# Five small moves in the routing work beside an attention loop on one Trainium2 core

## The chip, the core and the metric

The kernel runs on one core of one Trainium2 chip. TensorE (PE in the profile, with PEld for its weight loads), VectorE (DVE), ScalarE (ACT), GpSimd (POOL) and the DMA queues (SP's and others) each work through their own list of instructions in order, and wait for each other through semaphores. The metric is the device time of one execution in microseconds (us); lower is better.

## The reference

Two blocks follow each other. The first is a linear attention with a decaying state, for 4 batches, 8 heads, 768 tokens and 48 values a head; the second routes each token to one of 8 experts and applies that expert.

```
# attention, for every batch and head, t = 0..767
y[t]  = r[t] @ (state + (u*k[t])^T v[t]);  state = w[:,None]*state + k[t]^T v[t]
x     = y of the 8 heads side by side               # (4, 768, 384)
# routing and experts
logits = x @ w_gate (8 experts);  local = sigmoid(x @ w_local)
fresh  = argmax(logits)                              # first of equals
e[s]   = fresh if s == 0 or local < 0.5 else e[s-1]  # else keep the last token's expert
p      = softmax(logits)[e];  out = p * (relu(x @ w1[e]) @ w2[e])     # 384 -> 1024 -> 384
```

## The kernel before

**The attention loop.** `Attention.run` goes over 16 items (batch by head pair: n = 4*batch + pair, two heads at a time on 128 partitions) and one closing step. An item has 6 chunks of 128 tokens. Step n of the loop finishes item n-1 and begins item n, and it already computes the scores of item n+1. What belongs to one item:

- `load`: three DMAs on SP's queue (`rk`, `kv`, `vT`), four items ahead.
- `scale` on POOL: `rw` (r by powers of the decay), `ke` (k by powers of the decay), `pd` (r times k), two instructions each, one step ahead of their use. `keys` on DVE: `kw`, two steps ahead.
- `scores` on PE (L288), in two halves into two PSUM tiles of two banks each (`pair0`, `pair1`), which are taken in turn by everything that needs a bank; DVE masks each half into `am` (L290) and so frees the bank.
- `own` on PE (L267) into `y`, then DVE multiplies it by `vT` (L273). `inside` (L297) and `before` (L310) add the other two parts to `y`; ACT copies it to `xT` (L318). `turn` (L329) transposes it back into token order, and ACT copies that to `x` (L331).
- `added` on PE (L248) writes the states that the chunks add into `T`, and `states` on DVE (L254, a scan) runs over `T` and gives `S`, which `before` needs.

**The routing of the first two batches** ("group 0", 12 chunks) is put in pieces into steps 9 to 15 of the same loop (`g` is 8 in the code). `logits` and `token_logits` give `lt` at steps 8, 9, 12 and 13. `experts_of` finds the argmax (L688 to L696: maximum, comparison `eq`, product with `down`, maximum, key), `keys` transposes the keys (L703), `runs` is a running maximum that carries an expert forward (L708), `turn_runs` and `last` go back (L713, L720), `one_hot` ends it (L727 to L731). `counts` (L740, L741, PE) and `ranks` (L747 on ACT, L748 to L756 on DVE) number the tokens of each expert; `slots`, `columns` (`eqv`, L800), `places` (`ohq`, L811, two halves) and `numbers` (`val`, L805 on POOL) build the one-hot tables from which `summed` (L818, PE) makes the list of tokens for the first two experts. `head` (L828 to L849) ends with `gid`, by which POOL gathers rows of x from DRAM (L1077). After the loop the expert units follow, each a run of matmuls; they route the other two batches on their way.

**One PSUM bank for much.** `mp` is a single bank. It holds the tables of the first steps (columns 0 to 256), `T` (columns 258 to 497), the maximum `mx`, the transposed keys, and behind `T` (`mp[:, mp_end:]`) what `turn_runs` and `last` write. The tile library adds the semaphore waits, and it keeps two engines off one bank at the same time: a matmul that writes into `mp` waits for the DVE reads of `mp` that stand in front of it in the program, whatever their columns are.

**The order** is written out by hand: inside `tc.manual_schedule()` every engine's list has its instructions in the order in which the Python code issues them. So moving a line of `run` moves its instructions on each engine that it uses, and nothing else decides. `iota` makes small integer tables on POOL, and `cast` at step 6 turns some of them into floats on ACT.

Of the kernel before, what the change touches and what calls it, by code (L numbers as in the profile page):

```python
# [14 lines left out]
Alu = mybir.AluOpType  # L15
# [5 lines left out]
P = 128  # L21
# [5 lines left out]
E, F = 8, 1024  # L27
DK, FK = D // P, F // P
NCH = S // P
NC = B * NCH  # L30
N = B * S

ST = 4
# [4 lines left out]
EARLY = 2  # L38
HEAD = 192
TAIL = 256  # L40
# [15 lines left out]
def spread(ap, axis, n):  # L56

    a = ap.unsqueeze(axis)
    return a.to_broadcast([n if i == axis else s for i, s in enumerate(a.shape)])


class Attention:
# [289 lines left out]
    def run(self, router, fetch, heads):  # L352


        def pair(name):
            t = self.banks(name)
            return [t[:, 0], t[:, 1]]

        M = B * HP

        mp, mp_end = router.mp, 2 * P + 2 + (NCH - 1) * DH

        g = GROUPS[0][1] * HP
        for n in range(M + 1):
            if n + AHEAD - 1 < M:
                self.load(n + AHEAD - 1)
            if n == 0:
                self.scale(0)
                self.keys(0)
                self.tables()  # L370
                self.scores(0, 0)()
                self.scores(0, 1)()
                self.own(0)
                self.nc.scalar.copy(self.first, self.tab[:, 1, 0])
                self.turn_ends(slice(1, HP))
                self.warm(3)
                self.added(0)
                self.reciprocals(1)
                self.states(0)
                self.scale(1)  # L380
                continue
            if n < 3:

                self.keys(n)
                self.inside(n - 1)
                self.before(n - 1)
                if n == 2:
                    self.turn(0, pair("tp"))
                self.nc.scalar.copy(self.first, self.tab[:, n + 1, 0])
                self.scores(n, 0)()  # L390
                keep = self.scores(n, 1)
                self.own(n)
                keep()
                self.added(n)
                self.states(n)
                if n == 1:
                    self.reciprocals(2)
                self.scale(n + 1)
                continue
            if n < M:  # L400
                self.turn(n - 2, pair("tp"))
                if n >= M - 2:
                    fetch(2 * (n - M + 2))
                if n == 3:
                    self.reciprocals(3)
                if n < 5:
                    self.keys(n)
                if n > 3:
                    if n not in (g + 3, g + 5):
                        self.added(n)  # L410
                    self.states(n)
            if n == 4:
                self.keys(5)
            if n > HP and n % HP == 1:
                self.token_logits(n // HP - 1, pair("lq")[0])
            if n == g + 1:
                router.experts_of(0, (0,))
            if n == g + 5:
                router.slots(0)
                router.columns(0)  # L420
            if n == M:
                router.shares(0)
            if n + 1 < M:
                self.scale(n + 1)
            if n == g + 6:
                router.numbers(0, self.nc.gpsimd)
            if 3 <= n < 6:
                router.constants(n - 3)
            if n == M:
                self.turn(M - 2, [self.spare[:, 0], self.spare[:, 1]])  # L430
            self.inside(n - 1)
            if n == g + 3:

                router.turn_runs(0, mp[:, mp_end:])
            self.before(n - 1)
            if M - 2 <= n < M:
                fetch(2 * (n - M + 2) + 1)
            if n == 6:
                router.cast()
            if n == M:  # L440
                break
            if n == g + 3:
                router.last(0, mp[:, mp_end:])
                router.one_hot(0, (0,))
            if n == g + 7:

                router.summed(0, 0)
                router.copied(0, self.nc.vector.tensor_copy)
                self.spare = self.py.tile([P, 2, 512], F32, name="y")
                router.head(self.spare[:, 0])  # L450
                heads()

            ahead = n if n < 5 else n + 1
            if n == 3:
                self.added(3)
                self.states(3)
            if ahead < M:
                self.scores(ahead, 0)()
                keep = self.scores(ahead, 1)
            if n % HP == 0:  # L460

                keep()
                self.own(n)
                self.logits(n // HP - 1, pair("lp")[0])
                if n == 4:
                    self.scores(5, 0)()
                    self.scores(5, 1)()
                    self.keys(6)
                if n == g + 4:
                    self.added(n + 1)  # L470
                    router.counts(0, [mp, mp[:, E * NC // 2:]])
                    router.ranks(0, (0,))
                if n > 4:
                    self.keys(n + 2)
                if n == g + 4:
                    router.ranks(0, (1,))
            else:
                self.own(n)
                if n == g + 2:
                    self.added(n + 1)  # L480
                    router.keys(0, mp)
                    router.runs(0)
                if 4 < n < M - 2:
                    self.keys(n + 2)
                if ahead < M:
                    keep()
            if n == g + 1:
                router.experts_of(0, (1,))
            if n == g + 3:
                router.one_hot(0, (1,))  # L490
            if n == g + 5:
                router.places(0, 0)
            if n == g + 6:
                router.places(0, 1)
        self.inner.close()
# [81 lines left out]
class Router:  # L577
# [43 lines left out]
    def iota(self, name, shape, pattern, base=0, cm=0, cast=False):  # L621
# [5 lines left out]
        self.casts.append((f, i))  # L627
        return f

    def constants(self, part):  # L630
        nc = self.nc
        if part == 0:
            self.ie = self.iota("ie", [P, E], [[1, E]])
            self.iq = self.iota("iq", [P, P], [[1, P]])
            self.ij = self.iota("ij", [P, E * ST], [[1, E * ST]])
            self.ones = self.tl("r_ones", [P, P])
            nc.vector.memset(self.ones, 1.0)
        elif part == 1:
            self.down = self.iota("down", [P, E], [[-1, E]], base=E, cast=True)

            self.t8 = self.iota("t8", [P, NC], [[E * P, NC]], base=2 * E, cm=E, cast=True)
            self.t1 = self.iota("t1", [P, NC], [[P, NC]], base=1, cm=1, cast=True)
        else:

            c = self.g[0]["nc"]
# [5 lines left out]
            nc.vector.memset(self.go, 1.0)  # L651
            nc.vector.memset(self.go.rearrange("p (b c) -> p b c", c=NCH)[:, :, NCH - 1:], 0.0)
            nc.vector.memset(self.g[0]["ext"][:, :, 0:1], 0.0)

            self.tie = self.tl("tie", [P, E])
            for x, (z, base) in enumerate(((slice(0, EARLY), E - 1 - E * TAIL), (slice(EARLY, E), E - 1 - EARLY))):
                i = self.iota(f"tie{x}", [P, z.stop - z.start], [[-1, z.stop - z.start]], base=base)
                self.casts.append((self.tie[:, z], i))
            self.ief = self.iota("ief", [1, E], [[1, E]], cast=True)

            self.size = self.tl("size", [1, E])
            for i, n in enumerate(BLOCKS):
# [18 lines left out]
    def experts_of(self, i, parts=(0, 1)):  # L681

        nc, g, lt = self.nc, self.g[i], self.lt
        lg = lt[:, g["z"], :E]
        if 0 in parts:
            nc.vector.memset(lt[:, g["z"]].rearrange("p (b c) e -> p b c e", c=NCH)[0:1, :, 0, E:], -1.0)
            mx = self.mp[:, :g["nc"]] if i == 0 else g["mx"]
            nc.vector.tensor_reduce(mx, lg, axis=AX.X, op=Alu.max)  # L688
            nc.vector.tensor_tensor(g["eq"], lg, spread(mx, 2, E), op=Alu.is_equal)
            if i == 0:  # L690
                nc.scalar.copy(g["mx"], mx)
            nc.vector.tensor_tensor(g["eq"], g["eq"], spread(self.down, 1, g["nc"]), op=Alu.mult)
        if 1 in parts:
            nc.vector.tensor_reduce(g["k"], g["eq"], axis=AX.X, op=Alu.max)
            nc.vector.tensor_tensor(g["k"], self.t8[:, g["z"]], g["k"], op=Alu.subtract)
            nc.vector.scalar_tensor_tensor(g["key"], lt[:, g["z"], E], FRESH_TO, g["k"],  # L696
                                           Alu.is_le, Alu.mult)
# [1048 lines left out]
```

## Time and profile before

| what | value |
|---|---|
| time, 3 runs | median 382.65 us (382.16 to 382.88) |
| the profiled execution | 383.9 us, of which its span is 382.2 us |
| PE busy / PE weight loads | 367.5 us (96%) / 324.1 us (85%) |
| DVE / ACT / POOL busy | 250.6 us (66%) / 107.5 us (28%) / 151.3 us (40%) |
| attention loop | about 0 to 112 us of the span |
| expert units | about 112 to 373 us, PE busy throughout |

The profiled execution took 1.25 us more than the median of the timed runs. Times in the text are microseconds from the start of the span. A step of the loop is read best from one `before` (L310) to the next on PE. Busy PE does not mean PE at full rate: the granted clock of the array is given beside it.

### The profile page before, as it was taken

The page shows a single profiled execution, that of the slowest core. Times are in us where ns is not written, and L with a number is a line of the kernel's source. Part 1 is how long each engine was busy: PE and PEld are TensorE (multiplying, and loading weights), DVE is VectorE, ACT ScalarE, POOL GpSimd, SP SyncE. Part 2 cuts the span into 40 slices and gives each one's busy share as a digit, 9 for nine tenths or more (in the row PEclk, how much of TensorE's full clock was granted, in tenths as well). Part 3 has the DMA queues.
Part 4 walks back from the last instruction along what each step waited for, and adds up shares of the span by engine and source line. Part 5 has one row for each costly group of instructions (what it writes and reads, how often), then busy time and mean ns, then how long its engine had stood idle before and what let it go on. Part 6 is the DMA issues. An engine that isn't in the chain of part 4 may idle for free. (4 is left out here: it accounts for less than half of the span.)

```text
span 382.2 us, 9693 instructions
## 1 busy us (share of the span) xinstructions
PE 367.5 (96%) x3846; PEld 324.1 (85%) x3846; DVE 250.6 (66%) x720; ACT 107.5 (28%) x295; POOL 151.3 (40%) x213
## 2 busy tenths in 40 slices
PE   7999999989999999999999999999999999999992
PEld 6776777766769998999999999999998899899971
DVE  6888778967945746496566857758758758466400
ACT  4132232223222212322422333233234233232210
POOL 8779999867222042311422313212323113012022
PEclk9999999989999999999999999999999999999997
DMA  7999999972566881720551254145246156064011
GB/s 262 409 410 410 408 396 327 358 272 91 189 223 209 317 352 41 306 107 22 211 204 62 63 190 192 51 173 207 76 166 228 37 178 228 10 215 170 3 37 36
DMA packets 17765, 74.97 MB, mean 196 GB/s; under 512 B 2761, under 2 KB 6618, under 8 KB 15408
## 3 DMA queue, kind: packets, MB, share of 16 engines
q1 hardware_dynamic: 10336, 56.89, 39.9%
q0 software_dynamic: 3424, 9.52, 7.5%
q10 hardware_dynamic: 3952, 7.87, 5.7%
q8 instruction: 32, 0.52, 0.5%
q14 instruction: 21, 0.17, 0.1%
HBM read 64.83 MB, written 9.51 MB: 195 GB/s over the span
## 5 line engine op out<-in xcount | busy, mean ns | idle before, releaser
L1303 POOL DMA_INDIRECT out_dram<-yo,sid x27 | 26.6, 987 | 102.4 <-ACT yo L1298 79.0
L1154 PE MATMUL h<-exT,w1t 128*128 128x168 f32 (+4 forms) x240 | 54.9, 327 | 0.0
L1158 DVE TENSOR_TENSOR hT<-h,hs 128x168 f32<-128x168 f32 (+3 forms) x60 | 21.1, 351 | 46.5 <-PE h L1154 31.0
L1077 POOL DMA_INDIRECT xg<-x_d,gid x29 | 31.1, 1073 | 37.1 <-DVE sm L900 17.4
L1154 PEld LDWEIGHTS h<-exT,w1t 128*128 128x128 f32 x240 | 41.6, 190 | 0.3 <-issue 0.3
L1104 PE MATMUL h<-exT,w1t 128*128 128x192 f32 (+1 forms) x192 | 38.3, 338 | 0.0
L1223 PE MATMUL y<-factors,sums 128*128 128x192 f32 x168 | 36.8, 326 | 0.0
L216 POOL TENSOR_TENSOR pd<-rk 128x384 f32<-128x384 f32 x32 | 31.3, 999 | 10.2 <-PE y L267 7.6
L1154 PE MATMUL h<-xs,ws 128*128 128x168 f32 (+4 forms) x144 | 35.2, 326 | 0.0
L290 DVE TENSOR_TENSOR am<-pair,kept 128x768 f32<-128x768 f32 x32 | 30.0, 951 | 6.7 <-PE pair L288 6.1
L1104 PEld LDWEIGHTS h<-exT,w1t 128*128 128x128 f32 x192 | 32.3, 190 | 1.5 <-issue 0.2
L1154 PEld LDWEIGHTS h<-xs,ws 128*128 128x128 f32 x144 | 25.5, 190 | 4.3 <-ACT hs L1161 1.2
L1223 PEld LDWEIGHTS y<-factors,sums 128*128 128x128 f32 x168 | 28.9, 190 | 0.0
L212 POOL TENSOR_TENSOR ke<-kv,endT 128x288 f32<-128x288 f32 x32 | 25.0, 800 | 0.7 <-DMA kv<-in_kv_dram 0.7
L297 PE MATMUL y<-am,kv 128*64 128x128 f32 x360 | 23.9, 276 | 0.8 <-DVE y L273 0.8
L288 PE MATMUL pair<-rw,kw 48*64 48x128 f32 (+1 forms) x768 | 23.2, 253 | 1.4 <-DVE lt L349 0.6
L229 POOL TENSOR_TENSOR rw<-rk,tab 128x384 f32<-128x384 f32 x26 | 23.5, 924 | 2.1 <-DMA rk<-in_rk_dram 2.1
L1223 PE MATMUL y<-w2t,hT 128*128 128x192 f32 x96 | 23.0, 328 | 0.0
L288 PEld LDWEIGHTS pair<-rw,kw 48*64 48x64 f32 x768 | 19.7, 135 | 3.6 <-issue 1.2
L1091 DVE COPY exT<-tp 128x384 f32<-128x384 f32 (+6 forms) x29 | 14.0, 488 | 12.9 <-PE tp L1090 12.7
L297 PEld LDWEIGHTS y<-am,kv 128*64 128x64 f32 x360 | 20.0, 137 | 2.4 <-DVE y L273 1.0
L318 ACT COPY xT<-y 128x768 f32<-128x768 f32 x15 | 12.0, 801 | 34.0 <-PE y L310 34.0
(300 smaller groups left out, 740.4 us busy)
## 6 DMA issues: line engine op xcount, KB each, us to landing
w1t<-in_w_dram SPq DMA_DIRECT2D x8, 1536.0 KB, 6.6
w2t<-in_w_dram SPq DMA_DIRECT2D x8, 1536.0 KB, 7.1
rk<-in_rk_dram SPq DMA_DIRECT2D x15, 768.0 KB, 9.9
kv<-in_kv_dram SPq DMA_DIRECT2D x16, 584.0 KB, 8.4
vT<-in_vT_dram SPq DMA_DIRECT2D x16, 384.0 KB, 7.8
x_d<-x ACTq DMA_DIRECT2D x4, 1152.0 KB, 8.2
w1t<-in_w_dram SPq DMA_DIRECT2D x2, 768.0 KB, 4.6
w2t<-in_w_dram SPq DMA_DIRECT2D x2, 768.0 KB, 5.3
```

What stands on the lines that cost most here:

```text
L212: nc.gpsimd.tensor_mul(t["ke"][:, p::2], t["k"][:, p::2], spread(self.endT[:, p, hp], 1, C2))
L216: nc.gpsimd.tensor_mul(t["pd"][:, z], t["rT"][:, z], t["kT"][:, z])
L229: engine.tensor_mul(t["rw"][:, z], t["rT"][:, z], spread(pw, 1, z.stop - z.start))
L288: nc.tensor.matmul(sc[f * DP:(f + 1) * DP, h, i, x:], lhsT=t["kw"][q, c, o * DP:(o + 1) * DP], rhs=t["rw"][q, c, x:], start=True, stop=True)
L290: return lambda: nc.vector.tensor_mul(t["am"][:, g], sc, spread(self.kept[:, g:g + 3], 1, 2))
L297: nc.tensor.matmul(t["y"][h][p * DP:(p + 1) * DP, c2 * P:(c2 + 1) * P], lhsT=t["v"][:, (2 * c + h) * DH:(2 * c + h) * DH + DP], rhs=t["am" ...
L1077: self.nc.gpsimd.indirect_dma_start(out=xg[:n], out_offset=None, in_=self.x_d[:rows], in_offset=bass.IndirectOffsetOnAxis(ap=u["gid"][:n, ...
L1104: nc.tensor.matmul(h[:, :n], lhsT=u["w1"][:, m, kk, :], rhs=u["xT"][:, kk, :], start=(kk == 0), stop=(kk == DK - 1))
L1154: nc.tensor.matmul(out, lhsT=a, rhs=b, start=start and k == 0, stop=stop and k == len(terms) - 1, skip_group_check=True)
L1158: nc.vector.tensor_tensor(out, a, b, op=Alu.add)
L1223: return lambda: nc.tensor.matmul(bank[:, x * half:(x + 1) * half], lhsT=a, rhs=b, start=(j == 0 and x == 0), stop=(j == FK // 2 - 1), ski ...
L1303: self.nc.gpsimd.indirect_dma_start(out=out.rearrange("n (h d) -> (n h) d", h=2) if half else out, out_offset=bass.IndirectOffsetOnAxis(ap ...
```

## The change

Five moves, no new arithmetic:

1. In `experts_of` for group 0, the comparison `eq` is written into columns 12 to 107 of `mp` (PSUM), and its product with `down` reads it there; the product goes to the same SBUF tile as before.
2. The state scan of step 11 (`states(11)`) is issued in step 10, right behind `runs`, in place of its position at the start of step 11. On DVE it now stands in front of `kw` of item 12 and of the second `am` of item 11.
3. At step 12 `added(13)` and `counts` are issued in front of `logits` instead of behind it. `ranks` stays behind `logits`, so on ACT the copy `lT` of `logits` stays in front of the copy `ext` of `ranks`.
4. `eqv` moves from the start of step 13 to its end; the first half of `ohq` moves from the end of step 13 to step 14, behind its scan.
5. All nine `iota` tables are made on POOL at the end of step 2, in front of `scale(3)`, instead of in steps 3, 4 and 5.

```diff
@@ Attention.run
                 if n == 1:
                     self.reciprocals(2)
+                else:
+                    router.numbering()
                 self.scale(n + 1)
...
-                    self.states(n)
+                    if n != g + 3:
+                        self.states(n)
...
             if n == g + 5:
                 router.slots(0)
-                router.columns(0)
...
             if n == g + 6:
                 router.numbers(0, self.nc.gpsimd)
-            if 3 <= n < 6:
+                router.places(0, 0)
+            if n in (3, 5):
                 router.constants(n - 3)
...
                 self.own(n)
+                if n == g + 4:
+                    self.added(n + 1)
+                    router.counts(0, [mp, mp[:, E * NC // 2:]])
                 self.logits(n // HP - 1, pair("lp")[0])
...
                 if n == g + 4:
-                    self.added(n + 1)
-                    router.counts(0, [mp, mp[:, E * NC // 2:]])
                     router.ranks(0, (0,))
...
                     router.keys(0, mp)
                     router.runs(0)
+                    self.states(n + 1)
...
             if n == g + 5:
-                router.places(0, 0)
+                router.columns(0)
@@ Router (numbering() holds the iotas that constants() had)
+    def numbering(self):
+        self.ie = self.iota("ie", [P, E], [[1, E]])
+        self.iq = self.iota("iq", [P, P], [[1, P]])
+        self.ij = self.iota("ij", [P, E * ST], [[1, E * ST]])
+        self.down = self.iota("down", [P, E], [[-1, E]], base=E, cast=True)
+        self.t8 = self.iota("t8", [P, NC], [[E * P, NC]], base=2 * E, cm=E, cast=True)
+        self.t1 = self.iota("t1", [P, NC], [[P, NC]], base=1, cm=1, cast=True)
...
@@ Router.experts_of
-            nc.vector.tensor_tensor(g["eq"], lg, spread(mx, 2, E), op=Alu.is_equal)
+            eq = self.mp[:, g["nc"]:g["nc"] * (E + 1)].rearrange("p (c e) -> p c e", e=E) if i == 0 else g["eq"]
+            nc.vector.tensor_tensor(eq, lg, spread(mx, 2, E), op=Alu.is_equal)
             if i == 0:
                 nc.scalar.copy(g["mx"], mx)
-            nc.vector.tensor_tensor(g["eq"], g["eq"], spread(self.down, 1, g["nc"]), op=Alu.mult)
+            nc.vector.tensor_tensor(g["eq"], eq, spread(self.down, 1, g["nc"]), op=Alu.mult)
```

## The prediction

> **What bounds the kernel now.** I read the stages first (busy time by window: PE, weight loads, DVE, ACT, POOL, granted PE clock, DMA share, GB/s).
>
> ```profile
> 28.00:66.00 38.00, 37.16 (x814) 27.48 (x804) 30.01 (x59) 9.85 (x26) 38.00 (x52) 1.00 1.00 387
> 66.00:112.00 46.00, 42.48 (x889) 32.55 (x886) 36.27 (x59) 11.99 (x30) 28.56 (x33) 0.96 0.69 239
> 112.00:382.00 270.00, 262.82 (x1675) 243.92 (x1671) 161.78 (x557) 76.37 (x217) 63.78 (x89) 0.99 0.41 145
> ```
>
> From 112 us on PE never stops until the last sends, so whatever the loop ends earlier moves all of that forward. From 28 to 66 us PE has 0.84 us of gaps, though POOL is busy throughout: POOL is ahead (`rw(8)` ends at 51.39, its scores start at 54.10). All edits but the table move lie in 64 to 108 us, where PE has gaps and the clock falls below 1. The timelines of PE and DVE there (start, us, engine, line, what, idle before and its releaser):
>
> ```profile
> 69.46 0.80 PE L329 MATMUL pair<-ident,xT 112*128 112x112 f32 x6 [0.65 <-DVE am L290]
> 78.60 0.23 PE L713 MATMUL mp<-ident,run 12*128 12x12 f32 x1 [1.00 <-DVE inc L726]
> 95.55 0.77 PE L288 MATMUL pair<-rw,kw 48*64 48x128 f32 x24 [0.63 <-DVE lt L349]
> 97.69 0.79 PE L329 MATMUL pair<-ident,xT 112*128 112x112 f32 x6 [0.73 <-DVE am L290]
> ...
> 65.57 0.25 DVE L689 TENSOR_TENSOR eq<-lt,mp 128x96 f32<-128x96 f32 x1
> 65.86 2.67 DVE L692 TENSOR_TENSOR eq<-eq,down 128x96 f32<-128x96 f32 x1
> 68.46 0.94 DVE L290 TENSOR_TENSOR am<-pair,kept 128x768 f32<-128x768 f32 x1
> 75.87 0.40 DVE L708 TENSOR_TENSOR_SCAN run<-mp,seg 12x128 f32<-12x128 f32 x1
> 76.20 0.92 DVE L236 TENSOR_TENSOR kw<-rk,inv 128x768 f32<-128x768 f32 x1
> 77.05 0.94 DVE L290 TENSOR_TENSOR am<-pair,kept 128x768 f32<-128x768 f32 x1
> 77.92 0.63 DVE L254 TENSOR_TENSOR_SCAN S<-step,mp 128x240 f32<-128x240 f32 x1
> ...
> 116.14 0.26 DVE L692 TENSOR_TENSOR eq<-eq,down 128x96 f32<-128x96 f32 x1
> ```
>
> Three things are to be seen. L692 takes 2.67 us at 65.86 and 0.26 at 116.14, with the same shape. L713 starts when the scan S has ended (78.55), not when `run` has (76.27): it writes the bank that S reads; the name L726 is only DVE's next instruction. And DVE runs without a pause from 64.31 to 78.56, so there its order decides. The clock stands right behind L713's gap:
>
> ```profile
> 79.00:80.00 1.00, 1.00 (x26) 0.83 (x25) 0.00 (x0) 0.33 (x2) 1.00 (x2) 1.00 1.08 353
> 80.00:81.00 1.00, 1.00 (x42) 1.00 (x46) 0.76 (x4) 0.72 (x2) 0.06 (x1) 0.77 0.89 347
> 81.00:82.00 1.00, 1.00 (x22) 0.61 (x16) 0.72 (x1) 0.00 (x0) 0.00 (x0) 0.50 1.00 413
> 82.00:83.00 1.00, 1.00 (x9) 0.21 (x2) 0.04 (x1) 0.00 (x0) 0.00 (x0) 0.50 0.88 361
> 83.00:84.00 1.00, 1.00 (x6) 0.83 (x5) 1.00 (x2) 0.00 (x0) 0.98 (x2) 0.52 0.28 105
> 84.00:85.00 1.00, 1.00 (x29) 0.94 (x30) 1.00 (x2) 0.70 (x2) 1.00 (x3) 1.00 0.19 22
> ```
>
> **Comparison in PSUM (step 9).** During L692 POOL runs `rw` and `ke` without a break:
>
> ```profile
> 65.23 1.67 POOL L229 TENSOR_TENSOR rw<-rk,tab 128x384 f32<-128x384 f32 x2
> 66.88 1.54 POOL L212 TENSOR_TENSOR ke<-kv,endT 128x288 f32<-128x288 f32 x2
> 68.99 1.96 POOL L216 TENSOR_TENSOR pd<-rk 128x384 f32<-128x384 f32 x2 [0.57 <-PE y L267]
> ```
>
> L692 ends at 68.53, just after POOL's fourth instruction (68.42). `kw`, with one operand in PSUM, takes 0.92 to 0.95 beside POOL everywhere. So with `eq` in PSUM L692 costs about 0.26. New: it has to wait for ACT's copy of `mx` out of the same bank (65.92 to 66.09), so it ends near 66.45. The next `am` then waits for PE: its scores start at 66.67, and `am` follows them by 0.87 in the quiet steps (48.53 to 49.40), so 67.54 instead of 68.46. L329 starts behind L267 at 68.74 instead of 69.46: 0.72 for PE. DVE keeps 0.39 of it, as `y` waits for L267 (68.94 instead of 69.33). Next come L695 and L696, both with two SBUF inputs, 0.73 and 0.72 us beside POOL (72.19, 72.95) and 0.17 each at 116.72. Arriving 0.39 earlier they meet POOL's `rw` pair at another place: if L695 slips in between its two (71.88), `S(10)` is 0.7 earlier; if both wait as now, L696 ends at 73.67 as now, `S(10)` holds up L248 and `y` holds up L297 (76.06), and nothing is left. I take 0.35 at L297, bounds 0 and 0.75. A worse lock is the second rival.
>
> Here a rule speaks. The Trainium skill ("SBUF — State Buffer", Who interferes with whom) says that a DVE instruction with two SBUF inputs and a GpSimd instruction that reads SBUF exclude each other, for the whole instruction. The trace agrees on who is hit, but L692 waited across four POOL instructions. By the rule it would get in when the first of the `rw` pair ends (66.07) and end near 66.3, ahead of its need; then this edit is worth 0, not 0.35. The measured row decides for the profiled execution, but other executions may differ, hence the lower bound.
>
> **Scan behind the runs (step 10).** `added(11)` (L248, 74.70) is done before `run` starts, so S can follow `run` at once: 76.2 to 76.9. L713 then waits only for its turn behind L297 (76.06 plus 1.5, so 77.55): 1.05 from the move, plus the 0.35 above: 1.40 (bounds 1.05 and 1.80). On DVE `kw(12)` and `am` now end 0.58 later, `am` at 78.2 to 78.6; it frees the bank for the next L288, which comes at 78.5 behind L720: no wait, or 0.1. On ACT `rn` and `xT` follow L713 and L310 as before.
>
> **The clock.** From L288 (79.91) to L248 (84.06) PE takes 4.15 us. The same pieces in quiet steps are 1.27 (72.62 to 73.89), 0.80 and 0.73 (49.81, 50.61, 51.34): 2.80. So the slow period costs 1.35 if it is there, and 0 if not. The Trainium skill ("TensorE: Matmul & The Clock Gate", What's actually happening) says the clock halves only after an idle window of about 3.4 us. The trace shows 0.50 for about that long, but after a gap of only 1.00 us. By the rule the gap isn't the cause, the edit saves none of it, and the sum is 1.5; by the trace it stands right behind the gap and goes with it, and the sum is 2.85. Against the trace: 94.10 to 97.50 us has less PE busy (2.24 us of 3.40) and stayed at 1.00.
>
> **Counts ahead of logits (step 12).** The counts end 1.42 us earlier on PE (L342's length, 88.58 to 90.00), but `ext` stays behind `lT` on ACT, which now waits for the later logits: about 91.63 instead of 91.31, a loss of 0 to 0.32 for L748 and the DVE chain behind it, which ends in `lt` and L288's wait of 0.63. L748 took 1.08 (0.37 at 126.04) because it waited for POOL's `rw` until 92.40; an arrival 0.3 later meets the same end. I take 0.1 lost.
>
> **`eqv` and `ohq` (steps 13, 14).** L800 (0.56) leaves the place in front of `am`: L329's 0.73 falls by 0.48. But DVE is full from 91.58 to 101.7, and L800 still stands ahead of the next `am` (101.72, freeing the bank at 102.68; L329 takes it at 102.93). So PE arrives 0.48 earlier and waits 0.25 again: 0.2 stays. POOL's `val` (0.83) now starts only after L800 (about 100.2) and can hold `ohq` 0.3. L818, at 106.52, needs `val` much later. Net 0.2, bounds -0.1 and 0.4.
>
> **Tables (step 2).** Nine iotas, 0.41 + 0.29 + 0.26 = 0.96 us of POOL, move into a pause: POOL waits 2.08 us for the `rk` load before 21.79. Gain 0, as POOL has 2 us in hand at steps 4 to 9; loss 0, unless that load came over 1 us earlier. `cast` needs them at 49.65. No DMA, and nothing of SP's queue, is moved.
>
> **Sum** against the profiled 383.9 us: 1.40 + 1.35 - 0.10 + 0.20 + 0 = 2.85, so 381.05. The median of the runs shown is 382.65, 1.25 lower. That is almost the 1.35 of the slow period, as if those runs hadn't it; it may as well be the cost of profiling. Their spread (0.72) says that they are of one kind, not of which. I charge half, 0.7, to the timed median: 1.50 + 0.7 = 2.2, so 380.5.
>
> **Rivals.**
> 1. The waits go, but the timed runs have no slow period to lose, or keep it: 1.5 off, 381.2 (bounds 380.8 to 381.9). For it: the 1.25 and the rule. Against: the profile's only slow period before the end stands behind the gap.
> 2. The lock moves on to L695 and L696. If, like L692, L695 isn't let in until POOL's fourth instruction ends (74.39), POOL goes straight on with `pd` (L267 has released it) and L696 waits until 76.3. `S(10)` ends 2.8 us later than now, PE stands still from 73.98 to 77.0, L297 comes at 78.4 and L713 at 79.95, 1.35 later than now, with the slow period kept: 384.0. It turns to a loss once the two take over 2.7 us together (1.45 now), for then L297 ends after 78.6. For it: 2.67 at L692. Against: the two got in at POOL's boundaries.
> 3. Nothing measurable: DVE's locks and the later `ext` use up what L713 gives: 382.3.
>
> **How the numbers follow.** Waits and slow period both gone or partly (379.2 to 380.8): 0.47. Rival 1: 0.32. Rival 3: 0.10. Rival 2: 0.11. The range 379.0 to 382.1 holds the first two and half of the third. A run of this kernel can tell about 0.2% (0.77 us) from no change: faster, below 381.88, 0.78; same 0.11; slower 0.11.
>
> **Right or wrong.** Right: L692 near 0.3 us; no 0.65 at step 9's L329; no gap at L713, whose releaser is now L297; PEclk 1.00 in 78 to 84 us; iotas at 19.7 to 20.7. Wrong: L695 and L696 longer than 2 us together; `exc` later against L342 and a PE wait over 0.9 at `lt`; a slow clock at another gap; `am` in front of L288 holding PE at step 11.

## The result, and the profile after

The changed kernel was compared with the one before on three occasions: 382.29 us against 382.90 (ratio 0.9975, 95% interval 0.9962 to 0.9988), 381.71 against 382.52 (0.9971, 0.9956 to 0.9986), and 381.34 against 382.63 (0.9970, 0.9954 to 0.9986). So it is faster by 1.0 to 1.1 us by the ratios, 0.6 to 1.3 by the medians. Forecast were 2.2 us, and 382.29 lies above the range of 379.0 to 382.1; 0.25 us of that is the level, since the kernel before took 382.90 beside it and 382.65 when the forecast was made. The sign was right, the size twice too big.

The first profiled execution of the change took 382.2 us with a span of 380.4 us (before: 383.9 and 382.2). Its stages (columns as in the prediction: PE, weight loads, DVE, ACT, POOL, granted clock, DMA share, GB/s):

```profile
66.00:112.00 46.00, 44.16 (x917) 33.16 (x914) 35.14 (x62) 13.11 (x33) 27.50 (x31) 1.00 0.69 244
```

PE is busy for 1.68 us more of these 46 us than before, at a clock of 1.00 instead of 0.96. The places that the prediction named, on DVE and on PE:

```profile
66.32 0.26 DVE L697 TENSOR_TENSOR eq<-mp,down 128x96 f32<-128x96 f32 x1 [0.29 <-ACT mx L696]
78.74 0.95 DVE L733 TENSOR_TENSOR ei<-inc,rn 128x12 int32<-128x12 f32 x1
...
68.93 0.79 PE L329 MATMUL pair<-ident,xT 112*128 112x112 f32 x6
77.04 0.23 PE L718 MATMUL mp<-ident,run 12*128 12x12 f32 x1
93.06 0.77 PE L288 MATMUL pair<-rw,kw 48*64 48x128 f32 x24 [0.42 <-DVE lt L349]
100.44 0.80 PE L329 MATMUL pair<-ident,xT 112*128 112x112 f32 x6 [0.59 <-DVE am L290]
```

The waits that the first two edits were to remove are gone: the product of `eq` takes 0.26 us, L329 in step 9 follows without a pause, L718 (L713 before) follows L297. L288 waits 0.42 us for `lt` instead of 0.63, and the 0.73 of L329 in step 13 has no counterpart any more. But two things are new: `ei` takes 0.95 us, and PE waits 0.59 us for `am` in step 14. All five signs by which the prediction wanted to be known as right can be seen in this profile, the clock of 1.00 among them. They say nothing of whether the timed runs before had a slow clock to lose.

### The profile page after: what moved, and what is told of

The parts are those of the page before. It is cut to its first block, busy times and chain, and to the rows that moved or that the text cites. A ratio compares the mean times of both kernels' runs of the same rounds, so it can differ in the third digit from the quotient of the medians.

```text
span 380.4 us, 9693 instructions
## 1 busy us (share of the span) xinstructions
PE 366.9 (96%) x3846; PEld 323.9 (85%) x3846; DVE 248.7 (65%) x720; ACT 107.1 (28%) x295; POOL 151.3 (40%) x213
## 3 DMA queue, kind: packets, MB, share of 16 engines
q10 hardware_dynamic: 3952, 7.87, 5.7%
## 5 line engine op out<-in xcount | busy, mean ns | idle before, releaser
L288 PE MATMUL pair<-rw,kw 48*64 48x128 f32 (+1 forms) x768 | 23.5, 249 | 1.3 <-DVE lt L349 0.4
L297 PE MATMUL y<-am,kv 128*64 128x128 f32 x360 | 23.9, 276 | 0.8 <-DVE y L273 0.8
L288 PEld LDWEIGHTS pair<-rw,kw 48*64 48x64 f32 x768 | 19.6, 133 | 3.8 <-issue 2.1
L297 PEld LDWEIGHTS y<-am,kv 128*64 128x64 f32 x360 | 20.0, 137 | 2.4 <-DVE y L273 1.0
```

The lines of the kernel that those rows point to most:

```text
L288: nc.tensor.matmul(sc[f * DP:(f + 1) * DP, h, i, x:], lhsT=t["kw"][q, c, o * DP:(o + 1) * DP], rhs=t["rw"][q, c, x:], start=True, stop=True)
L297: nc.tensor.matmul(t["y"][h][p * DP:(p + 1) * DP, c2 * P:(c2 + 1) * P], lhsT=t["v"][:, (2 * c + h) * DH:(2 * c + h) * DH + DP], rhs=t["am" ...
```

## How the steps are compared

The reading that settled this case is the start of L329 in each step, which is PE's own clock for the loop. Below are the differences from one step to the next (step 8's L329 comes at 62.3 to 63.4 us in all profiles), then from step 14 to the first `h` matmul of the expert units, and the whole. "Before" stands for three profiles of the same kernel, "change" for three as well; the other rows are told below. The profile of e_scan, in which PE stood still for 5.38 us in step 9, is left out.

| kernel (profile) | 8-9 | 9-10 | 10-11 | 11-12 | 12-13 | 13-14 | 14-h | 8-h |
|---|---|---|---|---|---|---|---|---|
| before, first | 6.57 | 5.93 | 7.41 | 8.31 | 6.58 | 5.24 | 12.29 | 52.33 |
| before, second (b_again) | 5.86 | 5.99 | 6.28 | 7.77 | 6.49 | 5.24 | 12.27 | 49.90 |
| before, third (b_third) | 6.39 | 6.13 | 6.38 | 7.77 | 6.50 | 5.24 | 12.35 | 50.76 |
| change, first | 5.85 | 5.98 | 5.91 | 7.87 | 5.85 | 5.90 | 12.15 | 49.51 |
| change (a_again) | 5.85 | 5.98 | 5.91 | 7.87 | 5.82 | 5.89 | 12.23 | 49.55 |
| change (a_third) | 5.85 | 5.98 | 5.90 | 7.88 | 5.84 | 5.90 | 12.16 | 49.51 |
| e_warm | 6.15 | 5.93 | 7.29 | 7.78 | 6.49 | 5.25 | 12.27 | 51.16 |
| e_psum | 5.85 | 6.24 | 6.26 | 7.78 | 6.48 | 5.24 | 12.35 | 50.20 |
| e_nocnt | 5.85 | 5.97 | 5.92 | 7.77 | 5.94 | 5.90 | 12.26 | 49.61 |
| e_noeqv | 5.85 | 6.16 | 5.89 | 7.91 | 6.60 | 5.24 | 13.93 | 51.58 |
| e_ext | 5.86 | 5.98 | 5.91 | 7.86 | 5.41 | 5.89 | 12.38 | 49.29 |
| e_ei | 5.85 | 6.44 | 5.61 | 7.87 | 5.82 | 5.90 | 12.48 | 49.97 |
| e_both | 5.85 | 5.98 | 5.71 | 7.87 | 5.38 | 5.90 | 12.33 | 49.02 |
| e_ohq | 5.86 | 5.97 | 5.92 | 7.87 | 5.81 | 5.24 | 12.60 | 49.27 |
| e_best | 5.85 | 5.98 | 5.91 | 7.87 | 5.43 | 5.24 | 12.64 | 48.92 |
| e_best2 | 5.86 | 5.97 | 5.70 | 7.87 | 5.39 | 5.24 | 12.60 | 48.63 |
| e_best3 | 5.86 | 5.98 | 5.81 | 7.91 | 5.50 | 5.24 | 13.14 | 49.44 |

The first pair differs by 2.82 us at the loop's end, almost the 2.85 of the forecast sum; that the two agree is luck in part, as the terms below show. The other two profiles of before are 0.39 and 1.25 slower than the change there, one on either side of the timed 1.0 to 1.1.

One caution: column 9-10 isn't equal in kernels that do the same there. It is 0.15 to 0.46 longer in b_third, e_psum, e_noeqv and e_ei, where L267 on PE takes 1.06 to 1.33 us instead of 0.88. This comes in the kernel before as in the changed one, so it belongs to no edit; its cause is open.

## The experiments

Times are medians; ratios are to the kernel before run beside them, with their 95% interval.

**The two kernels again.** No edit.

> The kernel before, unchanged, once more. Theory A (the timed executions of the kernel before have no slow-clock period; the profiled one was unlucky or disturbed): this second profile shows a granted clock of 1.00 from 78 to 86 us, or a slow period somewhere else, and L713's gap of about 1.0 us without it. Theory B (the slow period belongs to the gap and is in every execution): granted clock 0.5 for about 3.4 us right behind the gap again. Both: timed ratio 1.000 within 0.002. ScalarE's activation at about 141.5 us comes at once behind its matmuls, as in the first profile.

> The changed kernel, once more. Its first profile led by 2.6 us at the end of the loop and lost 0.85 of it at 140.9 us, where an activation of ScalarE (hT) started 2 us after its matmuls. Theory C (that stall belongs to the change): it is there again at the same place. Theory D (it is an accident of one execution): it is elsewhere or absent, and the lead of 2.6 us lasts to the end. Timed: 0.9975 again within 0.0015 by either.

> The kernel before as it is, a third look. If the slow clock behind L713's gap is an accident of the first profile, the granted clock is 1.00 in 78 to 86 us with the gap of about 0.9 us present, and the span is 379.8 to 380.3 us; if it comes and goes with the length of L692's wait, it is there only if L692 takes 2.5 us or more.

b_again: 382.30 us (0.9995, 0.9975 to 1.0014), profiled span 380.0. a_again: 381.71 us (0.9971), span 379.5. b_third: one execution, 382.5 us, span 380.7. First b_again, the timelines of DVE and PE, then its windows at the place where the clock fell to 0.50 in the first profile:

```profile
66.15 1.60 DVE L692 TENSOR_TENSOR eq<-eq,down 128x96 f32<-128x96 f32 x1
78.12 0.23 PE L713 MATMUL mp<-ident,run 12*128 12x12 f32 x1 [0.90 <-DVE inc L726]
79.83 0.17 DVE L728 TENSOR_TENSOR ei<-inc,rn 128x12 int32<-128x12 f32 x1
```

```profile
81.00:82.00 1.00, 1.00 (x10) 0.58 (x6) 0.81 (x2) 0.00 (x0) 0.51 (x1) 1.00 1.00 403
82.00:83.00 1.00, 1.00 (x31) 0.98 (x32) 1.00 (x2) 0.70 (x2) 1.00 (x2) 1.00 0.34 140
```

The same of b_third:

```profile
65.96 2.48 DVE L692 TENSOR_TENSOR eq<-eq,down 128x96 f32<-128x96 f32 x1
69.37 0.80 PE L329 MATMUL pair<-ident,xT 112*128 112x112 f32 x6 [0.47 <-DVE am L290]
78.70 0.23 PE L713 MATMUL mp<-ident,run 12*128 12x12 f32 x1 [1.00 <-DVE inc L726]
```

```profile
81.00:82.00 1.00, 1.00 (x23) 0.35 (x13) 0.82 (x1) 0.03 (x1) 0.00 (x0) 1.00 0.87 356
82.00:83.00 1.00, 1.00 (x23) 0.86 (x25) 0.98 (x2) 0.29 (x1) 0.93 (x1) 1.00 0.57 228
```

The gap in front of L713 is there both times, about as long as in the first profile, and the sixth number behind the window's length, the granted clock, stays at 1.00. So the gap by itself doesn't bring the slow period, and a wait of 2.48 us at L692 doesn't either. How often an execution has one can be read from the mean granted clock of the whole span, which is listed for every timed execution. It was 0.989 in the first profile of before, 0.996 and 0.995 in these two. Of 203 executions of before in four comparisons, 16 had 0.989 or less (four in each comparison), and they took 384.1 to 389.0 us. So a lower clock recurs, in about one execution in twelve, and the median doesn't have it. None of the 66 executions of the change was below 0.992, where five or so would be expected at the rate of before: the change seems to remove the low clock from those few executions. Where in them it lies, and which edit does it, isn't shown; e_scan and e_psum, with one edit each, still have one such execution of 16 and of 14.

L692 varies from one execution to the next: 2.67, 1.60 and 2.48 us. At 1.60 PE does not notice; at 2.48 it waits 0.47.

**e_warm: the gap at L713 filled.** The kernel before, with eight idle matmuls into unused columns of `y`'s banks in front of L713 (cut):

```
+ y = self.items[n - 1]["yy"]
+ for i in range(8):
+     nc.tensor.matmul(y[:, i % 2, C2 * P:], lhsT=self.ident, rhs=self.ident, start=False, stop=True, ...)
```

> Nothing is moved; eight idle matmuls (about 0.9 us) into unused columns of y's bank fill L713's gap, so PE is busy while it waits for the scan. No wait is shortened. Theory A: no timed gain (1.000). Theory B: the slow period behind the gap goes with the idle time, timed gain about 1.3 us (0.9966), and the profile shows a granted clock of 1.00 from 78 to 86 us with L713 still at about 78.6.

383.29 us (1.0018, 0.9998 to 1.0037). The filler was too long: it took 2.05 us and pushed L717 (L713 before) 1.03 us back (79.15 against 78.12), with the clock at 1.00. The +0.7 us is about what that push costs alone. Had every execution of before lost 1.35 us to the clock, the sum would have been a gain of 0.3. The two repeats above say the same more cleanly.

**e_scan: the scan's move alone.** `states(11)` behind `runs`, nothing else.

```
-                    self.states(n)
+                    if n != g + 3:
+                        self.states(n)
...
                     router.runs(0)
+                    self.states(n + 1)
```

> Only the scan of step 11 is moved behind the running maximum. L713's gap of 1.0 us goes (start 77.6 instead of 78.6), L692 keeps its 2.7 us. Theory A: timed gain about 1.0 us (0.9974). Theory B: the slow period goes too, timed gain about 2.4 us (0.994).

382.28 us (0.9991, 0.9969 to 1.0013): unresolved. Its profiled execution took 389.2 us, with L692's product (L694 here) at its longest. The timelines of DVE, PE and POOL in e_scan, and a window:

```profile
65.70 7.41 DVE L694 TENSOR_TENSOR eq<-eq,down 128x96 f32<-128x96 f32 x1
74.03 1.38 PE L329 MATMUL pair<-ident,xT 112*128 112x112 f32 x6 [5.38 <-DVE am L290]
...
69.16 1.93 POOL L216 TENSOR_TENSOR pd<-rk 128x384 f32<-128x384 f32 x2
71.06 1.93 POOL L229 TENSOR_TENSOR rw<-rk,tab 128x384 f32<-128x384 f32 x2
76.53 1.54 POOL L212 TENSOR_TENSOR ke<-kv,endT 128x288 f32<-128x288 f32 x2 [3.54 <-issue]
```

```profile
74.00:76.00 2.00, 1.97 (x22) 1.69 (x24) 2.00 (x3) 0.55 (x2) 0.00 (x0) 0.50 0.15 14
```

The product ended at 73.11, only when POOL had nothing more to run (72.99). Here PE stood still for 5.38 us, and the clock was 0.50 right behind it, for about six microseconds (74 to 80 us). So the slow clock followed the long gap here, and didn't follow the gaps of 0.9 to 1.0 us in the repeats of before.

**e_psum: `eq` in PSUM alone.** Edit 1 of the change.

> The kernel before with one edit: group 0's eq lies in PSUM (step 9). The multiply by down (L693 here) should take 0.26 us, as in the changed kernel, instead of 2.67 or 1.60. Theory A (the lock's long wait is rare, and the usual 1.6 us is absorbed: in the repeat of before, L329 came at 69.03 with no gap): the median within 0.2 us of before, only the slowest runs gone (worst below 384 instead of 385 to 388). Theory B (the prediction's 0.35 at L297): 0.35 us faster. L713's gap of 0.9 to 1.0 near 78 us stays, and ei takes 0.17 us at 79.8, since the scan still stands in front.

381.88 us (0.9979, 0.9954 to 1.0004), span 380.0 as b_again; the product takes 0.26 us. The median is within noise of before. The tail that this edit was to cut was not cut: the slowest of its 14 runs took 388.25 us, the slowest of before beside it 386.93. So the longest executions have another cause than L692's wait, and that half of theory A falls. What the edit saves in a given execution is the difference of column 8-9: 0.01 against b_again, 0.54 against b_third.

**e_nocnt and e_noeqv: one part of the change taken back.** Counts behind the logits again; or `columns` in front and `places(0, 0)` at the end of step 13 again.

> The changed kernel with one edit taken back: the counts stand behind the logits on PE again. The prediction's term says that this is 0.1 us better (ACT then copies ext 0.3 us earlier, behind an earlier lT); the stretch from L329 in step 9 to L329 in step 14 would be 31.4 instead of 31.50 us. If the wait for lt grows instead (0.53 in the kernel before against 0.38 to 0.42), the edit was worth about 0.1 us by itself.

> The changed kernel with one edit taken back: eqv stands in front of step 13's am again and the first half of ohq at the end of step 13. If eqv and ohq are worth what the prediction gave them (0.2), the stretch from L329 in step 9 to L329 in step 14 grows from 31.50 to 31.7 us, with a wait of 0.74 in step 13 and none in step 14; theory D (0.74 against 0.59, so 0.1 to 0.2) says the same. If the edit is worth nothing or costs, the stretch is 31.5 or less. The time should stay within 0.3 us of the changed kernel.

e_nocnt: 381.78 us (0.9980, 0.9966 to 0.9995). Without the counts' move step 11-12 is 0.10 shorter and 12-13 is 0.10 longer, so from step 9 to step 14 it is 31.50, as in the change: the move is worth nothing. PE waits 0.66 for `lt` instead of 0.38 to 0.42, because it comes there earlier. e_noeqv: 381.63 us (0.9982, 0.9966 to 0.9997). Its stretch from step 9 to 14 is 31.80, 0.30 longer than the change's, of which 0.18 lies in step 9-10, ahead of the edit; 0.1 is the edit's. Its profiled span, 383.6, has a wait of 1.59 us for the gather of `xg` (0 to 0.26 in the others) and loses as much again behind the loop; it isn't used.

**e_ext: ACT takes the counts at once.** The changed kernel, with ACT's copy `ext` taken out of `ranks` into a function `extend` of its own and issued right behind `counts`:

```
                     router.counts(0, [mp, mp[:, E * NC // 2:]])
+                    router.extend(0)
                 self.logits(n // HP - 1, pair("lp")[0])
```

> The changed kernel, with ACT's copy ext (L752) moved from behind lT (L343) to right behind the counts. Theory A (moving the counts on PE was no use because ACT took them in the old order): ext ends near 87.2 us instead of 89.3, DVE's idle time of 1.93 us in front of exc shrinks to under 0.3, the wait of 0.38 to 0.42 us of L288 for lt goes, and L329's wait of 0.59 in step 14 goes at least in part: 0.4 to 0.9 us faster than the changed kernel. Theory B (DVE's locks with POOL use the time up, or PE waits for another thing next): within 0.2 us of the changed kernel.

381.06 us (0.9965, 0.9951 to 0.9978). ACT and DVE of e_ext:

```profile
87.28 0.24 ACT L751 COPY ext<-mp 128x96 f32<-128x96 f32 x1 [2.17 <-PE mp L747]
87.55 0.89 DVE L759 TENSOR_TENSOR_SCAN exc<-seg,ext 128x104 f32<-128x104 f32 x1
89.99 0.73 DVE L766 TENSOR_TENSOR pos<-pos,far 128x24 f32<-128x24 f32 x1
90.75 0.80 DVE L767 TENSOR_TENSOR pos<-pos,oh 128x96 f32<-128x96 f32 x1
```

`ext` is ready 1.8 us earlier than in the change, DVE's idle time of 1.93 us in front of `exc` and PE's wait for `lt` are gone, step 12-13 is 0.43 shorter. Part is handed back: the products of `pos` now meet POOL and take 0.73 and 0.80 us, against 0.18 and 0.26 in the change. The wait of 0.58 in step 14 stays.

**e_ei and e_both: `ei` with one input in PSUM.** The changed kernel, and e_ext, with group 0's `inc` in free columns of `mp`:

```
+        if i == 0:
+            g["inc"] = self.mp[:, P + 8:P + 9 + g["nc"]]
```

> The changed kernel, with group 0's inc in unused PSUM columns, so that ei (L733) has one SBUF input. Theory A (ei's wait for POOL hands back part of L718's gain): ei takes about 0.2 instead of 0.95 us, am behind it starts near 79.1 instead of 79.7 to 79.8, L329 in step 11 doesn't wait for it, and the lead on the kernel before grows by 0.3 us. Theory B (PE's own L288 and L267 are late there, by 0.27 us, and what is gained is lost again at lt): ei is short and the time stays within 0.15 us.

> Both edits: inc in PSUM and ext's copy right behind the counts. If the two losses are separate, their gains add up: 0.7 to 1.2 us faster than the changed kernel, 1.3 to 1.9 faster than the kernel before. If DVE's locks with POOL meet another instruction instead (ohq, oh, exc), less than 0.4 us faster than the changed kernel.

e_ei 381.42 us (0.9973, 0.9956 to 0.9990), e_both 381.16 us (0.9964, 0.9950 to 0.9978). DVE of e_ei:

```profile
79.00 0.17 DVE L735 TENSOR_TENSOR ei<-mp,rn 128x12 int32<-128x12 f32 x1
79.20 0.51 DVE L736 TENSOR_SCALAR ei<-ei 128x12 int32<-128x12 int32 x1
79.63 0.94 DVE L290 TENSOR_TENSOR am<-pair,kept 128x768 f32<-128x768 f32 x1
```

`ei` is short as expected, but the next instruction, which has one input, takes 0.51 instead of 0.17: part of the wait for POOL's `ke` (78.12 to 79.68) was passed on, and L329 in step 11 still waits 0.27 for `am`. The clock times mislead here, since this execution was 0.46 late from step 9-10 on, ahead of the edit. Counted from L720 (L718 in the change), `am` starts 2.48 us later, against 2.77 in a_again, and step 10-11 is 5.61 instead of 5.91: theory A's 0.3, in this step. In e_both it is 5.71, 0.2 less than in e_ext. In time nothing can be told: e_ei loses as much again behind step 14 (12.48), and e_both's median isn't below e_ext's.

**e_ohq, e_best, e_best2, e_best3: `ohq` out of the way of `am`.** In step 14 of the change, the first half of `ohq` moves behind the first `am`; e_best adds e_ext, e_best2 adds `inc` in PSUM as well. In e_best3 both halves of `ohq` stand at the step's end.

```
                 router.numbers(0, self.nc.gpsimd)
-                router.places(0, 0)
...
+                if n == g + 6:
+                    router.places(0, 0)
                 self.own(n)
```

> The changed kernel, with the first half of ohq (step 14) issued behind the step's first am and in front of y's multiply, instead of in front of that am. Theory A (the change only carried DVE's surplus from step 13 on to step 14, and there is a slot in which DVE would wait for L267 anyway): L329's wait of 0.59 us near 100.3 goes, ohq takes 0.95 instead of 1.31 us because val is over by then, y's multiply comes 0.3 to 0.5 us later than it could but not later than L297 needs it: 0.4 to 0.6 us faster than the changed kernel. Theory B (y becomes late and L297 waits instead, or L823 waits for ohq): within 0.2 us of it.

> The changed kernel with ext's copy right behind the counts and ohq's first half behind am. If the two losses are separate (0.38 at lt, 0.58 at L329), it is 0.8 to 1.0 us faster than the changed kernel, 1.4 to 2.0 us faster than before, with no wait of PE above 0.2 us between 64 and 103 us. If the lead runs into the gather of xg (L1101 waited 0.15 us for it in one run and 0.26 in another), 0.2 to 0.4 us of it are lost there.

> As the last one, with inc in PSUM as well. That edit by itself only passed the wait on from ei to the instruction behind it, so this should be within 0.15 us of the last one; if it isn't, the lock at step 11 is worth more than the profile shows.

> The changed kernel as it is, beside the three above on one chip. Expected: 0.6 to 1.0 us faster than before, waits of 0.38 to 0.42 us at L288 for lt and of 0.59 at L329 in step 14 again. If PE waits 0.5 us or more for ACT's hT near 141 us as in the first profile of the change, that is a part of the change and not an accident.

> As e_best2 (ext behind the counts, inc in PSUM), but both halves of ohq stand behind step 14's second am. If y's late multiply cost e_ohq and e_best2 0.3 us, L297 no longer waits in step 14, and the stretch from L329 in step 9 to the first h matmul, 42.77 us in e_best2, becomes about 42.5; the time is then 0.2 to 0.4 us below e_best2. If the product of val and ohq (L823 in the change) waits for ohq instead, it is equal or worse.

e_ohq 381.32 us (0.9953, 0.9933 to 0.9973), e_best 380.88 (0.9946, 0.9927 to 0.9966), e_best2 380.62 (0.9942, 0.9927 to 0.9957), a_third beside them 381.34 (0.9970), e_best3 in another comparison 381.57 (0.9975, 0.9958 to 0.9993). DVE and PE of e_best2 in step 14:

```profile
98.69 0.95 DVE L825 TENSOR_TENSOR ohq<-si,iq_i 128x768 f32<-128x768 int32 x1
100.56 1.53 PE L297 MATMUL y<-am,kv 128*64 128x128 f32 x24 [0.17 <-DVE y L273]
```

`ohq` takes 0.95 us, as `val` is over, and step 13-14 is back at 5.24. Of the 0.66, 0.44 go again (14-h is 12.60 instead of 12.16), most of it because `y` comes late: L297 starts 1.54 us behind L329 instead of 1.21. The losses at `lt` and at `am` are separate, and their repairs add up at step 14: 30.43 from step 9 for e_best, against 31.05 for e_ext, 30.81 for e_ohq and 31.50 for the change. e_best2 is 0.7 us under the change by median, 0.88 by 8-h, and the fastest version measured: 2.0 us under before by median. It was expected within 0.15 us of e_best and is 0.26 under it (0.29 by 8-h), so `inc` in PSUM is worth 0.2 to 0.3 in the trace here too; the intervals of the times overlap. e_best3 cures L297 (1.21 again) and loses more elsewhere. Its timelines of DVE and PE:

```profile
101.18 1.82 DVE L824 TENSOR_TENSOR ohq<-si,iq_i 128x768 f32<-128x768 int32 x2
102.92 0.65 DVE L254 TENSOR_TENSOR_SCAN S<-step,mp 128x240 f32<-128x240 f32 x1
103.71 0.86 PE L831 MATMUL mp<-ohq,val 128*32 128x128 f32 x24 [0.88 <-DVE S L254]
```

L831 needs `ohq`, ready at 103.00, but it writes `mp`, which the scan S reads until 103.57. A scan of `S` in the same bank is also what held L713 in the kernel before. The scan would have to stand in front of `ohq`, which wasn't tried.

## Why the prediction was wrong

**The clock: 1.35 in the sum and 0.7 of the forecast 2.2, 0 in the two repeats.** This is the step that failed. The prediction had the rule (the Trainium skill, "TensorE: Matmul & The Clock Gate", What's actually happening: an idle window of about 3.4 us) against a single trace and didn't settle which of them holds: it counted the slow period in full in the profile's sum, and charged half of it to the timed median. The repeats have the gap at L713 and no slow period, and only 16 of 203 timed executions of before have as low a mean clock as the first profile. The prediction's own clue, the 1.25 us between profile and median, fits: the median hadn't it. In the first profile the slow period cost about 1.6 us (7.41 and 8.31 in steps 10-11 and 11-12, against 6.28 to 6.38 and 7.77), so its size was nearly right, and only its place in the median was wrong. Without the term the sum is 1.50 and the forecast is rival 1's 381.2 (bounds 0.75 to 1.85 below before), which holds the measured 1.0 to 1.1. As to the rule: gaps of 0.90 and 1.00 us left the clock at 1.00 and one of 5.38 us was followed by 0.50, as it says; the first profile, with 0.50 behind a gap of 1.00, doesn't fit it, and what made the clock fall there is open.

**The gap at L713: 1.05 forecast, 0.97 at L718, about 0.4 behind it.** L713 comes 3.10 us behind step 10's L329 in b_again, L718 2.13 in a_again. But step 10-11 is only 0.37 to 0.48 shorter. This is the second term that was mis-sized. The prediction asked of the next `am` only whether it frees its bank, and found "no wait, or 0.1". It didn't follow the chain `inc`, `ei`, `am` in step 11. The timelines of DVE, PE and POOL in a_again:

```profile
78.60 0.95 DVE L733 TENSOR_TENSOR ei<-inc,rn 128x12 int32<-128x12 f32 x1
79.67 0.95 DVE L290 TENSOR_TENSOR am<-pair,kept 128x768 f32<-128x768 f32 x1
80.68 0.80 PE L329 MATMUL pair<-ident,xT 112*128 112x112 f32 x6 [0.33 <-DVE am L290]
77.96 1.57 POOL L212 TENSOR_TENSOR ke<-kv,endT 128x288 f32<-128x288 f32 x2
```

And of DVE and PE in b_again:

```profile
80.28 0.96 DVE L290 TENSOR_TENSOR am<-pair,kept 128x768 f32<-128x768 f32 x1
81.30 0.79 PE L329 MATMUL pair<-ident,xT 112*128 112x112 f32 x6
```

`ei` has both inputs in SBUF; a microsecond earlier it meets POOL's `ke` (77.96 to 79.53) and takes 0.95 instead of 0.17. So `am` starts 2.77 us behind L718, where it started 2.16 behind L713, and L329 starts 0.06 behind `am`'s end in both. These 0.61 us are what is lost of the 0.97. A second delay is hidden behind this one: on PE, L288 and L267 take 0.27 longer in a_again (78.21 to 80.36, against 79.43 to 81.31), and so much longer in the other two profiles of the change that L267 ends with `am` (80.77 and 80.76 in the first, 80.65 and 80.65 in a_third) and no wait is to be seen. Its cause is open, so a shorter `ei` alone would not always bring the 0.6 back; in e_ei, with L288 and L267 in time, it brought 0.3.

**`eq` in PSUM: 0.35 forecast, 0.01 to 0.72 measured.** By column 8-9 the edit is worth 0.01 against b_again, 0.54 against b_third and 0.72 against the first profile, in the order of L692's wait (1.60, 2.48 and 2.67 us). This is within the stated bounds (0 to 0.75), and right in mechanism. The rival in which the lock moves on to L695 and L696 didn't occur there: they take 1.06 us together in the changed kernel (L700 and L701), against 1.45 before. The lock moved to `ei`, and `ohq` now waits for `val` in step 14.

**Counts: -0.10 forecast, 0 measured.** The prediction noted that a later arrival of `exc` meets the same end of POOL's `rw`, and so it is: `exc` ends at 89.99 in e_nocnt and at 90.01 in a_again. It took off 0.1 all the same. That step 11-12 is 0.10 longer is a coincidence: on PE, L746 to L342 takes 0.32 us where L741 to L329 took 0.22, and step 12-13 gives it back. ACT's order made the move worthless, as e_ext shows by curing it.

**`eqv` and `ohq`: 0.20 forecast, about 0.1.** The prediction said that step 13's gain would be waited away at the next `am`, which is what happened: 0.66 off in 12-13, 0.66 on in 13-14. It added 0.2 that stays; 0.1 shows. It foresaw `val` holding `ohq`, with 0.3; `ohq` took 1.31 instead of 0.95.

**Tables: 0.** Right: the iotas ran at 19.69 to 20.64 in the first profile of the change, as forecast (0.8 later in a_again), and step 8's L329 comes at 62.94 to 63.08 us in the change, 62.89 to 63.17 before.

For the whole, by the table, a_third against b_again gives 0.01 + 0.01 + 0.38 - 0.11 + 0.65 - 0.66 + 0.11 = 0.39, against b_third 0.54 + 0.15 + 0.48 - 0.11 + 0.66 - 0.66 + 0.19 = 1.25. The timed gain lies between them, nearer to the upper one. The loop's lead is kept to the end, with one exception: in the first profile of the change PE waited behind the loop, where `hT` came late:

```profile
140.93 0.55 ACT L1112 ACTIVATE hT<-h 128x192 f32<-128x192 f32 x2 [4.66 <-PE h L1109]
141.31 1.24 PE L1196 MATMUL y<-hT,w2t 128*128 128x192 f32 x6 [0.58 <-ACT hT L1112]
```

In a_third the same L1196 starts at 140.45 without a wait, so this is no part of the change; its cause is open. Most of the difference between that profile's span of 380.4 and the 379.5 of the other two is this.

## What to carry to other kernels

Before a stage of a single trace is put into a sum, ask whether the timed runs have it: a second profile of the unchanged kernel would have taken out 1.35 of 2.85 here, and the granted clock of many timed executions tells how often such a period comes. Where an instruction comes earlier, follow its engine on to the next instruction that another engine waits for, and look up what POOL is doing at that new time. Moving work on one engine is worth nothing while the engine that takes the result stays in its old order (the counts and `ext`), and two edits that each only shift a surplus (`eqv`, `ohq`) are worth the slot that they find, not the wait that they remove.

## What was not expected of the hardware

A DVE product of 96 columns with both inputs in SBUF took 0.26 us alone and 1.60, 2.25 (in e_warm), 2.48, 2.67 and 7.41 us beside POOL, for the last across five groups of POOL instructions without a break (64.10 to 72.99 us). In all five profiles it ended 0.11 or 0.12 us behind the end of POOL's unbroken run: 67.75 and 67.64, 68.18 and 68.06, 68.44 and 68.33, 68.53 and 68.42, 73.11 and 72.99. So its length tells how far POOL was behind. In four of them `ke` ended before L267 had released POOL's next `pd`, and POOL paused; in e_scan `ke` ended at 69.19, L267 at 68.65, and POOL went straight on. The Trainium skill ("SBUF — State Buffer", Who interferes with whom) has the two exclude each other for one instruction; this product was held across two to nine. Others were let in while POOL went on, as L696 in b_again, here from the timelines of DVE and POOL:

```profile
72.31 0.89 DVE L696 SCALAR_TENSOR_TENSOR key<-lt,k 128x12 f32<-128x12 f32 x1
71.20 1.96 POOL L229 TENSOR_TENSOR rw<-rk,tab 128x384 f32<-128x384 f32 x2
73.13 1.55 POOL L212 TENSOR_TENSOR ke<-kv,endT 128x288 f32<-128x288 f32 x2
```

It ends at 73.20, as `rw` ends, with no pause of POOL before `ke`. What decides whether a waiting instruction is let in there isn't shown. With one input in PSUM the product took 0.26 us in every profile that has the edit. An instruction with a single SBUF input was also held: 0.51 us in e_ei and 0.60 to 0.62 in e_best2, e_both and e_best3, instead of 0.17, for the second instruction on `ei` (128x12, int32).
